# Regrouping a weight conversion beside a pooled attention: four visits per head pair behind the two result bursts, and doubled staging buffers

## The chip, the cores and the metric

One core of a Trainium2 chip runs the kernel. The metric is the device time of one execution in microseconds (us), median of the runs shown. Engines are called PE (TensorE), DVE (VectorE), ACT (ScalarE), POOL (GpSimd) and SP (SyncE, which here only issues DMAs).

## The reference, cut to what matters

```python
B, H, S, D = 8, 8, 1152, 64            # q, k, v: float32
q_pool = q.reshape(B, H, 576, 2, D).mean(axis=3)
scores = q_pool @ k.T / 8              # 576 x 1152 for each head
attn = softmax(scores)                 # stable: the row's maximum is subtracted
x = heads_side_by_side(attn @ v)       # 8 x 576 x 512
theta = x @ w_theta                    # 512 x 512
y = w_tok_r @ (x * cos(theta)) + w_tok_i @ (x * sin(theta))   # 576 x 576 each
u = x + y
out = u + relu(u @ w_ch)               # w_ch 512 x 512
```

The four weights arrive as float64. [...]

## The kernel before, in words

The kernel has two phases. Phase 1 is the attention, 32 pairs of heads (`NPAIR`); phase 2 is the rest, batch by batch. This case is about phase 1.

A pair has 18 positions, two halves `u` of nine `escore` steps. One step is eight short matmuls into a PSUM slot `pe` and an exponential by ACT (`pc`). PSUM has four slots (`bank2`), handed out in an order fixed when the program is written. The matmuls of later pairs are mixed in: `maxpass` (PE writes a slot `pm`, DVE reduces it to row maxima, `mx`), twelve times a pair. POOL adds the exponentials (`ssum`). Twice a pair comes a burst (`AV_AT`): 36 matmuls `pa` that multiply the exponentials with V.

- The burst of u = 0 stands at position 10.35. Ahead of its 36 matmuls PE transposes inputs of pair i+2 (`pt`); ACT makes the high part `hi`, DVE the low part `lo`. Behind them ACT copies the result (`xu`) and PE sums for the norm (`pns`). Call the place behind it A.
- The burst of u = 1 stands at 19.25, that is 1.25 of the next pair. Ahead of its matmuls come transposes for pair i+3 and `max_tail`, whose maxima DVE takes (`px`), then `hi` by ACT and `lo` by DVE. Call the place behind it C.

The row maxima next to C are at positions 2.45, 3.65 and 4.5 of a pair, next to A at 11.1, 12.35 and 13.45. Between burst and maxima stand `norm_out` (DVE, 10.5), `norm_store` (SP, 10.6), `norm_recip` (DVE, 1.5), `norm_save` and `norm_bcast` (SP, 1.6 and 1.7).

All engines run in the order of these positions: every function is put into a list with `at(position, priority, ...)`, the list is sorted, and each engine executes its instructions in just this order.

The weights are 18 blocks of up to 128 rows: four of `w_theta`, four of `w_ch`, five each of `w_tok_r` and `w_tok_i`, in turn. They go through a generator `wgen` that is advanced one step at each position in `W_AT`, nine a pair (20 a pair in the last two, `W_LAST`). A block takes 15 or 16 steps, so 1.7 pairs: fetch by DMA (`raw`), six DVE operations (L545 shift, L548 mask, L550 maximum, L552 shift and mask, L556 merge, L560 mask) with an ACT conversion (L547) behind the first, two POOL operations (L562, L564), nearly each in a step of its own; then the end: for `square` blocks a copy by ACT and a subtraction by POOL, for `token` blocks five PE transposes into a slot `pw`, two ACT copies and two DVE subtractions (L184). The staging tiles `raw`, `ws`, `wf` exist once.

Of the kernel before, what the change touches and what calls it, by code (L numbers as in the profile page):

```python
# [9 lines left out]
F32 = mybir.dt.float32  # L10
F32R = mybir.dt.float32r
# [3 lines left out]
ALU = mybir.AluOpType  # L15
# [5 lines left out]
MAX_AT = (-24.9, -23.65, -22.55, -20.85, -19.55, -18.8, -15.55, -14.35, -13.5, -11.6, -10.2, -9.15)  # L21
SS_LAG = 4.5
AV_AT = (10.35, 19.25)
W_FIRST = (9.45, 9.5, 9.85, 10.5, 12.75, 18.0, 18.6, 19.25, 20.45)
W_AT = (9.45, 9.5, 9.85, 10.5, 12.75, 18.0, 18.6, 19.25, 20.45)
W_LAST = (9.4, 10.2, 11.0, 11.8, 12.6, 13.4, 14.2, 15.0, 15.8, 16.6, 17.4, 18.2, 19.0, 19.8, 20.6, 21.4, 22.2, 23.0, 23.8, 24.6)
W_END = 30
PRO = ((-34.75, -25.8, -18.2), (-6.0, -5.0, 3.15), (3.75,))
MAX_AT0 = (-25.75, -25.25, -24.75, -24.25, -24.15, -23.25, -22.0, -21.95, -21.75, -21.25, -20.75, -20.25)
MAX_AT1 = (-18.1, -16.8, -16.1, -15.35, -14.7, -14.0, -13.3, -12.6, -11.7, -10.3, -9.8, -9.0)  # L30
# [61 lines left out]
TINY = 2.0**-15  # L92
# [9 lines left out]
def pooled_attention_moe_kernel(  # L102
# [24 lines left out]
    ND = DM // P  # L127
# [80 lines left out]
    with ExitStack() as p1:  # L208
# [305 lines left out]
            del state[i]  # L514

        def weights():
            wst = pw.enter_context(tc.tile_pool(name="wst", bufs=1, side="right"))
            wide = w_theta.dtype != F32

            def words(w):  # L520
# [2 lines left out]
                return w.bitcast(U32).rearrange("r (e o) -> r e o", o=2)  # L523

            def fetch(parts, n):
                ws = wst.tile([P, SQ], F32, tag="ws", name="ws")
# [5 lines left out]
                return raw, ws  # L532

            def narrow(raw, ws, R, n, g):
                dst = ws[0:R, 0:n].rearrange("a (t p) -> a p t", t=g)
                if not wide:
                    nc.vector.tensor_copy(
                        dst, raw[0:R, 0:n, 0].rearrange("a (p t) -> a p t", t=g)
                    )
                    return  # L540
                lo, hi = raw[0:R, 0:n, 0], raw[0:R, 0:n, 1]
                f = wst.tile([P, SQ], U32, tag="wf", name="wf")[0:R, 0:n]
                tl = lo.bitcast(F32)
                mk = ws[0:R, 0:n]
                nc.vector.tensor_scalar(lo, lo, 8, None, ALU.logical_shift_right)  # L545
                yield
                nc.scalar.activation(tl, lo, AF.Copy, scale=2.0**-44)  # L547
                nc.vector.tensor_scalar(f, hi, 0x7FFFFFFF, None, ALU.bitwise_and)  # L548
                yield
                nc.vector.tensor_scalar(mk, f.bitcast(F32), TINY, None, ALU.max)  # L550
                yield
                nc.vector.tensor_scalar(  # L552
                    f, mk.bitcast(U32), 3, 0x3FFFFFF8, ALU.logical_shift_left, ALU.bitwise_and
                )
                yield
                nc.vector.scalar_tensor_tensor(  # L556
                    f, hi, 0xC0000000, f, ALU.bitwise_and, ALU.bitwise_or
                )
                yield
                nc.vector.tensor_scalar(hi, f, 0xFF800000, None, ALU.bitwise_and)  # L560
                yield
                nc.gpsimd.tensor_tensor(tl, tl, hi.bitcast(F32), ALU.mult)  # L562
                yield
                nc.gpsimd.tensor_tensor(  # L564
                    dst,
                    f.bitcast(F32).rearrange("a (p t) -> a p t", t=g),
                    tl.rearrange("a (p t) -> a p t", t=g),
                    ALU.add,
                )
                yield  # L570

            def split_slow(hi, lo, src, eng):
                nc.scalar.copy(hi, src)
                yield
                eng.tensor_tensor(lo, src, hi.bitcast(F32), ALU.subtract)
                yield

            def square(wv, c, dst):
                yield
                raw, ws = fetch([(slice(0, P), wv[:, c])], DM)  # L580
                yield
                yield
                yield from narrow(raw, ws, P, DM, 1)
                yield
                if dst is None:
                    hl = [wst.tile([P, DM], F32R, tag=f"hl{n}", name="hl") for n in range(2)]
                    yield from split_slow(hl[0], hl[1], ws[:, 0:DM], nc.gpsimd)
                    yield
                    for n in range(2):
                        nc.sync.dma_start(wcd[n][c], hl[n].bitcast(F32))  # L590
                else:
                    yield from split_slow(dst[0][:, c], dst[1][:, c], ws[:, 0:DM], nc.gpsimd)
                yield

            def token(wv, kb, jt):
                R = P if jt < 4 else HT
                yield
                raw, ws = fetch([(dst, wv[t, ps]) for dst, t, ps in segments(jt)], SQ)
                yield
                yield  # L600
                yield from narrow(raw, ws, R, SQ, QT)
                yield
                yield
                yield
                pw2 = bank2("pw", "pwt")
                pt = pw2[:, 0]
                ra = 0 if kb == 0 else HT
# [14 lines left out]
                for dst, src in (  # L622
                    (
                        [w[:, kb : kb + 4, cs] for w in wtk],
                        pt.rearrange("a (j c) -> a j c", c=P)[:, :, 0:R],
                    ),
                    ([w[ra:rz, 8, cs] for w in wtk], ph[ra:rz, 0:R]),
                ):
                    split(dst[0], dst[1], src, nc.scalar, nc.vector)
                yield  # L630

            jobs = []
            for w, dst in ((w_theta, wth), (w_ch, None)):
                wv = words(w).rearrange("(c p) e o -> p c e o", p=P)
                jobs.append([square(wv, c, dst) for c in range(ND)])
            for w, kb in ((w_tok_r, 0), (w_tok_i, 4)):
                wv = words(w).rearrange("(p t) s o -> t p s o", t=QT)
                jobs.append([token(wv, kb, jt) for jt in range(5)])
            for n in range(5):
                for group in jobs:  # L640
                    if n < len(group):
                        yield from group[n]

        def early():
            run(wgen)
# [61 lines left out]
        pw = ExitStack()  # L707
# [4 lines left out]
            if c < ND - 1:  # L712
                at(XHI0_AT + 0.01 * c, 10, xlo, 0, c)
        for i in range(NPAIR):
            for pos in W_FIRST if i == 0 else W_AT if i < W_END else W_LAST:
                at(NU * i + pos, 10, next, wgen, None)
        for _, _, _, fn, args in sorted(todo, key=lambda e: e[:3]):
            fn(*args)
# [292 lines left out]
```

## Time and profile before

| | us |
|---|---|
| runs | 1395.92, 1396.42, 1396.66 (median 1396.42) |
| the profiled execution | 1395.23 |
| its span, first to last instruction | 1393.2 |
| granted clock over the span | 0.996 |

The profiled execution is longer than its span by 2.0 us, which lie outside the program's instructions. The attention takes the first 890 us or so of the span. Busy shares of the span are PE 96%, DVE 62%, ACT 52%, POOL 66%. "Busy" of an engine says little of a bound when an engine's instructions overlap each other; the waits and the starts of the bursts say more.

### The profile page before, as it was taken

The numbers are of one execution on the slowest core, as the hardware profiler recorded it, in microseconds if no ns is written. First come the engines' busy times: TensorE is split into PE (matmuls) and PEld (weight loads), VectorE is DVE, ScalarE is ACT, GpSimd is POOL, SyncE is SP. The second block draws the span as 40 slices with busy tenths as digits, with TensorE's granted clock in tenths as the row PEclk, the third lists the DMA queues.
The fourth block names the chain that finished last, engine by engine and source line by source line (L and its number), as shares of the span: only waits on it lengthen the run. The fifth ranks groups of instructions, "written<-read, shape, count | busy, mean of one in ns | idle before, by whom it ended". The sixth has DMA issues, their size and how long they took to land.

```text
span 1393.2 us, 29952 instructions
## 1 busy us (share of the span) xinstructions
PE 1342.4 (96%) x12178; PEld 1088.3 (78%) x12178; DVE 864.6 (62%) x1143; ACT 724.0 (52%) x1250; POOL 914.4 (66%) x672
## 2 busy tenths in 40 slices
PE   5999999999999999999999999899999999999998
PEld 3777777776777677777777777698999999999998
DVE  5867776776667776777677765465363453535442
ACT  1556565565556555565555565365454444445341
POOL 1789888989898998889898898742332322233220
PEclk9999999999999999999999999999999999999999
DMA  4334343334433444333443333221111211111111
GB/s 102 101 87 117 89 110 103 110 100 117 110 85 96 114 115 106 93 111 85 128 112 87 82 83 99 74 78 39 35 46 35 62 42 35 39 35 46 27 35 35
DMA packets 130906, 111.66 MB, mean 80 GB/s; under 512 B 95040, under 2 KB 95424, under 8 KB 130768
## 3 DMA queue, kind: packets, MB, share of 16 engines
q1 hardware_dynamic: 130592, 109.28, 28.9%
q8 instruction: 96, 1.57, 0.5%
q0 software_dynamic: 176, 0.46, 0.1%
q14 instruction: 42, 0.34, 0.1%
HBM read 88.29 MB, written 21.27 MB: 79 GB/s over the span
## 4 chain that ended last, share of the span: by engine, by line
PE 72%; DVE 15%; ACT 7%; DMA 3%; issue 2%; POOL 1%; SPq 0%; ACTq 0%; POOLq 0%; DVEq 0%
PE pe L390 18%; PE pa L411 17%; PE py L841 11%; PE pth L763 7%; PE pr L880 6%; DVE mx L332 5%; PE pt L285 4%; PE pm L325 3%; PE pns L427 2%; ACT pc L393 2%; PE pxn L751 1%; DVE r L785 1%; DVE r L786 1%; PE po L903 1%; DVE mx L351 1%
## 5 line engine op out<-in xcount | busy, mean ns | idle before, releaser
L402 POOL TENSOR_TENSOR ss<-ss,pc 128x576 f32<-128x576 f32 x384 | 561.8, 1463 | 68.9 <-ACT pc L393 45.8
L332 DVE TENSOR_REDUCE mx<-pm 128x2 f32<-128x768 f32 x384 | 347.5, 951 | 125.6 <-PE pm L325 124.0
L393 ACT ACTIVATE pc<-pe 128x576 f32<-128x576 f32 x576 | 364.8, 652 | 98.2 <-PE pe L390 85.6
L411 PE MATMUL pa<-pc,vn 128*64 128x288 f32 x2304 | 293.5, 409 | 0.9 <-PE pmt L362 0.8
L814 POOL TENSOR_TENSOR Z<-ab,Z 128x512 fp32r<-128x512 f32 x40 | 51.6, 1291 | 309.4 <-ACT Z L810 274.1
L411 PEld LDWEIGHTS pa<-pc,vn 128*64 128x64 f32 x2304 | 162.2, 137 | 109.4 <-issue 5.4
L841 PE MATMUL py<-wtk,Z 128*128 128x288 f32 x1728 | 242.0, 297 | 0.0
L841 PEld LDWEIGHTS py<-wtk,Z 128*128 128x128 f32 x1728 | 233.2, 189 | 1.5 <-ACT Z L810 0.2
L390 PE MATMUL pe<-hi 64*128 64x288 f32 x1152 | 202.7, 345 | 12.3 <-DVE mx L332 7.3
L390 PEld LDWEIGHTS pe<-hi 64*128 64x128 f32 x1152 | 109.5, 184 | 83.2 <-ACT pc L393 34.0
L390 PE MATMUL pe<-nmr,oner 64*128 64x288 f32 x1152 | 171.9, 291 | 2.2 <-DMA nmr<-mT 2.2
L390 PE MATMUL pe<-lo,hi 64*128 64x288 f32 x1152 | 172.2, 293 | 0.0
L390 PE MATMUL pe<-hi,lo 64*128 64x288 f32 x1152 | 172.0, 292 | 0.0
L325 PE MATMUL pm<-hi 64*128 64x384 f32 x768 | 137.5, 354 | 9.1 <-DVE mx L332 4.7
L390 PEld LDWEIGHTS pe<-nmr,oner 64*128 64x128 f32 x1152 | 110.5, 185 | 2.6 <-DMA nmr<-mT 2.6
L390 PEld LDWEIGHTS pe<-lo,hi 64*128 64x128 f32 x1152 | 111.0, 186 | 0.0
L390 PEld LDWEIGHTS pe<-hi,lo 64*128 64x128 f32 x1152 | 110.4, 185 | 0.0
L312 DVE TENSOR_TENSOR lo<-pt,hi 128x768 fp32r<-128x768 f32 x64 | 67.6, 1056 | 64.5 <-ACT hi L301 64.5
L880 PEld LDWEIGHTS pr<-us,wch 128*128 128x128 f32 x768 | 104.5, 188 | 2.0
L880 PE MATMUL pr<-us,wch 128*128 128x288 f32 x768 | 105.8, 295 | 0.0
L301 ACT CAST hi<-pt 128x768 fp32r<-128x768 f32 x64 | 56.2, 878 | 84.4 <-DVE mx L352 68.1
L402 POOL TENSOR_TENSOR ss<-pc,pc 128x576 f32<-128x576 f32 x64 | 93.8, 1466 | 5.9 <-ACT pc L393 5.9
(105 smaller groups left out, 1657.9 us busy)
## 6 DMA issues: line engine op xcount, KB each, us to landing
qn<-in_q_dram SPq DMA_DIRECT2D x32, 576.0 KB
kn<-in_k_dram SPq DMA_DIRECT2D x64, 288.0 KB
vn<-in_v_dram SPq DMA_DIRECT2D x32, 576.0 KB
dn<-ro SPq DMA_DIRECT2D x64, 144.0 KB
xd<-xu SPq DMA_DIRECT2D x32, 288.0 KB
xT<-xd SPq DMA_DIRECT2D x8, 1152.0 KB
out_dram<-on SPq DMA_DIRECT2D x23, 192.0 KB
out_dram<-on SPq DMA_DIRECT2D x23, 128.0 KB
```

Source lines behind the costliest of these rows:

```text
L285: nc.tensor.transpose(out=pt[:, n, c : c + R], in_=src.rearrange("p h d -> p (h d)"), identity=ident[0:R, 0:R],)
L301: nc.scalar.copy(hi, src)
L312: nc.vector.tensor_tensor(lo, src, hi.bitcast(F32), ALU.subtract)
L325: nc.tensor.matmul(pm[:, h, 0:W], hi[hs, Q0 + j * P : Q0 + (j + 1) * P], hi[hs, K0[3 * g] : K0[3 * g] + W], start=True, stop=True,)
L332: nc.vector.tensor_reduce(mx[:, j : j + 5 : 4, g : g + 1], pm[:, :, 0:W], AX.X, ALU.max)
L390: nc.tensor.matmul(pe[:, h, 0:HALF], w[hs], x[hs], start=(n == 0), stop=(n == 3))
L393: nc.scalar.activation(pcs[u, kt], pe[:, :, 0:HALF], AF.Exp, scale=SC)
L402: nc.gpsimd.tensor_tensor(st["ss", u], first, st["pc"][u, kt], ALU.add)
L411: nc.tensor.matmul(pa[hs, 0, 0:HALF], st["vn"][:, h, kt, :], st["pc"][u, kt][:, h, :], start=(kt == 0), stop=(kt == KT - 1),)
L763: nc.tensor.matmul(th, xs[c][:, j * P : (j + 1) * P], ws[:, c], start=(n == 0), stop=(n == 11))
L841: nc.tensor.matmul(st["py", c, u][:, 0:HALF], Z[zi][:, c * P : (c + 1) * P], wtk[wi][:, kw, u * HALF : (u + 1) * HALF], start=(i == 0 and ...
L880: nc.tensor.matmul(pr[u][:, 0:HALF], wch[wi][:, c, e * P : (e + 1) * P], st["us", ui][:, c, u * HALF : (u + 1) * HALF], start=(n == 0), st ...
```

## The change

- Four visits a pair, at 10.4 and 12.0 (A, and half a position behind one more `escore`) and at 19.3 and 20.9 (C, and the same behind it), take the place of nine, in all pairs alike.
- A block takes six visits (1.5 pairs). Its first: DVE operations shift, mask and maximum together, and the fetch of the next block. Its third: the ACT conversion and the other three DVE operations. Its fifth: both POOL operations. The second, fourth and sixth hold nothing of this.
- The end of a block runs beside the next block's visits: the ACT copy (or the PE transposes and both ACT copies) at that block's first visit, a token's DVE subtractions at its second, a square's POOL subtraction at its third.
- `raw`, `ws` and `wf` are doubled, and a block is fetched one block ahead.

The visits alternate: a block's first, third and fifth visits all fall to A or C. Blocks 0, 2, 4, ... have them at C, A, C; blocks 1, 3, 5, ... at A, C, A.

```diff
-W_FIRST = (9.45, 9.5, 9.85, 10.5, 12.75, 18.0, 18.6, 19.25, 20.45)
-W_AT = (9.45, 9.5, 9.85, 10.5, 12.75, 18.0, 18.6, 19.25, 20.45)
-W_LAST = (9.4, 10.2, 11.0, 11.8, 12.6, 13.4, 14.2, 15.0, 15.8, 16.6, 17.4, 18.2, 19.0, 19.8, 20.6, 21.4, 22.2, 23.0, 23.8, 24.6)
-W_END = 30
+W_AT = (10.4, 12.0, 19.3, 20.9)
...
-            wst = pw.enter_context(tc.tile_pool(name="wst", bufs=1, side="right"))
+            wst = pw.enter_context(tc.tile_pool(name="wst", bufs=2, side="right"))
...
                 nc.vector.tensor_scalar(lo, lo, 8, None, ALU.logical_shift_right)
+                nc.vector.tensor_scalar(f, hi, 0x7FFFFFFF, None, ALU.bitwise_and)
+                nc.vector.tensor_scalar(mk, f.bitcast(F32), TINY, None, ALU.max)
                 yield
                 nc.scalar.activation(tl, lo, AF.Copy, scale=2.0**-44)
-                nc.vector.tensor_scalar(f, hi, 0x7FFFFFFF, None, ALU.bitwise_and)
-                yield
-                nc.vector.tensor_scalar(mk, f.bitcast(F32), TINY, None, ALU.max)
-                yield
                 nc.vector.tensor_scalar(
                     f, mk.bitcast(U32), 3, 0x3FFFFFF8, ALU.logical_shift_left, ALU.bitwise_and
                 )
-                yield
                 nc.vector.scalar_tensor_tensor(
                     f, hi, 0xC0000000, f, ALU.bitwise_and, ALU.bitwise_or
                 )
-                yield
                 nc.vector.tensor_scalar(hi, f, 0xFF800000, None, ALU.bitwise_and)
                 yield
                 nc.gpsimd.tensor_tensor(tl, tl, hi.bitcast(F32), ALU.mult)
-                yield
                 nc.gpsimd.tensor_tensor(
...
+            def square(c, dst, ws):
...
+                nc.scalar.copy(hl[0], src)
                 yield
                 yield
-                yield from narrow(raw, ws, P, DM, 1)
+                nc.gpsimd.tensor_tensor(hl[1], src, hl[0].bitcast(F32), ALU.subtract)
+                yield
                 yield
                 if dst is None:
...
+                for (hi, lo), src in parts:
+                    nc.scalar.copy(hi, src)
                 yield
+                for (hi, lo), src in parts:
+                    nc.vector.tensor_tensor(lo, src, hi.bitcast(F32), ALU.subtract)
...
+            def step(steps):
+                steps[:] = [g for g in steps if next(g, "end") != "end"]
+
+            raws = [fetch(blocks[0][0], blocks[0][2])]
+            yield
+            yield
+            for n, (parts, R, cols, g, end) in enumerate(blocks):
+                step(ends)
+                ws = wst.tile([P, SQ], F32, tag="ws", name="ws")
+                body = narrow(raws[n], ws, R, cols, g)
+                next(body)
+                if n + 1 < len(blocks):
+                    raws.append(fetch(blocks[n + 1][0], blocks[n + 1][2]))
+                yield
+                step(ends)
+                yield
+                for _ in range(2):
+                    step(ends)
+                    next(body, None)
+                    yield
+                    step(ends)
+                    yield
+                ends.append(end(ws))
+            for _ in range(8):
+                step(ends)
+                yield
...
-            for pos in W_FIRST if i == 0 else W_AT if i < W_END else W_LAST:
+            for pos in W_AT:
                 at(NU * i + pos, 10, next, wgen, None)
```

## Rows read from the trace of the kernel before

**Rows 1.** The profile page, part 4: the chain of work that ended last, by engine.

```profile
PE 72%; DVE 15%; ACT 7%; DMA 3%; issue 2%; POOL 1%; SPq 0%; ACTq 0%; POOLq 0%; DVEq 0%
```

**Rows 2.** The same chain in order of time, whole span, pieces of bursts only: start in us, length in us, what. Those at 74.96, 127.45, 396.95, 425.68 and 831.41 are bursts of u = 0 (74.96 that of pair 1, 831.41 that of pair 29), the others of u = 1.

```profile
74.96 4.52 PE pa L411 x36
...
115.12 4.52 PE pa L411 x36
127.45 4.52 PE pa L411 x36
141.20 4.52 PE pa L411 x36
...
167.70 4.52 PE pa L411 x36
181.14 4.59 PE pa L411 x36
...
396.95 4.52 PE pa L411 x36
412.21 4.52 PE pa L411 x36
425.68 4.51 PE pa L411 x36
439.41 4.51 PE pa L411 x36
...
831.41 4.52 PE pa L411 x36
```

**Rows 3.** The timeline of DVE behind the burst at 115.12 (C, no weight operation near): start, length, instruction, and idle time before it with what ended it.

```profile
117.39 0.96 DVE L312 TENSOR_TENSOR lo<-pt,hi 128x768 fp32r<-128x768 f32 x1 [0.86 <-ACT hi L301]
118.26 0.20 DVE L451 RECIPROCAL rc<-rc 128x9 f32<-128x9 f32 x1
120.58 2.69 DVE L332 TENSOR_REDUCE mx<-pm 128x2 f32<-128x768 f32 x3 [2.12 <-PE pm L325]
```

**Rows 4.** The timeline of DVE behind the bursts at 412.21 and at 790.9 (both C), where a weight operation stands between the first row maximum and the second.

```profile
418.54 1.45 DVE L545 TENSOR_SCALAR raw<-raw 128x512 uint32<-128x512 uint32 x1
419.91 1.81 DVE L332 TENSOR_REDUCE mx<-pm 128x2 f32<-128x768 f32 x2
...
799.20 1.81 DVE L332 TENSOR_REDUCE mx<-pm 128x2 f32<-128x768 f32 x2
```

**Rows 5.** The timeline of PE in the same two places: the wait behind the first of them, and the burst before and after the second.

```profile
420.91 0.40 PE L390 MATMUL pe<-hi 64*128 64x288 f32 x2 [1.22 <-DVE mx L332]
...
790.92 0.95 PE L411 MATMUL pa<-pc,vn 128*64 128x288 f32 x6
...
804.90 0.70 PE L411 MATMUL pa<-pc,vn 128*64 128x288 f32 x3
```

**Rows 6.** Groups of instructions by line and shape, whole span: times found | busy us, mean ns of one | idle us before them, and what ended it. Six DVE operations of a block of 576 columns, then the ACT conversion, a token's larger DVE subtraction, `norm_out`, and POOL's sums.

```profile
L545 DVE TENSOR_SCALAR raw<-raw 128x576 uint32<-128x576 uint32 x8 | 6.7, 840 | 7.6 <-DMA raw<-in_moe_w_tok_i_dram 5.4 <-POOL ss L402 2.3
L548 DVE TENSOR_SCALAR wf<-raw 128x576 uint32<-128x576 uint32 x8 | 9.4, 1173 | 0.0
L550 DVE TENSOR_SCALAR ws<-wf 128x576 f32<-128x576 f32 x8 | 10.6, 1330 | 0.1
L552 DVE TENSOR_SCALAR wf<-ws 128x576 uint32<-128x576 uint32 x8 | 9.5, 1184 | 0.1
L556 DVE SCALAR_TENSOR_TENSOR wf<-raw,wf 128x576 uint32<-128x576 uint32 x8 | 11.8, 1480 | 0.1
L560 DVE TENSOR_SCALAR raw<-wf 128x576 uint32<-128x576 uint32 x8 | 5.4, 670 | 0.1
L547 ACT ACTIVATE raw<-raw 128x576 f32<-128x576 uint32 x8 | 5.9, 735 | 2.3 <-DVE raw L545 2.1
L184 DVE TENSOR_TENSOR wtk<-pwt,wtk 128x512 fp32r<-128x512 f32 x8 | 5.5, 691 | 10.8 <-ACT wtk L181 10.8
L473 DVE TENSOR_TENSOR xu<-xu,dn 128x576 f32<-128x576 f32 x32 | 35.8, 1119 | 15.2 <-DMA dn<-ro 15.2
L402 POOL TENSOR_TENSOR ss<-ss,pc 128x576 f32<-128x576 f32 x384 | 561.8, 1463 | 68.9 <-ACT pc L393 45.8
```

**Rows 7.** The timeline of DVE, three weight operations in a row ahead of the burst at 560.2 and one during the burst at 615.1, and that of POOL, the operation that waits for the latter one with its idle time before.

```profile
559.17 1.04 DVE L545 TENSOR_SCALAR raw<-raw 128x576 uint32<-128x576 uint32 x1
560.13 1.67 DVE L548 TENSOR_SCALAR wf<-raw 128x576 uint32<-128x576 uint32 x1
561.84 1.55 DVE L550 TENSOR_SCALAR ws<-wf 128x576 f32<-128x576 f32 x1
...
616.27 0.43 DVE L560 TENSOR_SCALAR raw<-wf 128x512 uint32<-128x512 uint32 x1
...
616.78 1.04 POOL L562 TENSOR_TENSOR raw<-raw 128x512 f32<-128x512 f32 x1 [1.56 <-DVE raw L560]
```

**Rows 8.** Busy time of the engines in six stretches of 4.2 to 4.3 us each that begin 3.2 to 3.3 us (C) or 2.1 us (A) behind the start of a burst, where `lo` ends when no weight operation is ahead of it: the sum and mean over six at C (from 118.35, 253.05, 305.55, 415.45, 632.10 and 686.00), then over six at A (from 129.60, 264.20, 290.70, 427.80, 643.30 and 670.90).

```profile
sum 25.50, PE 25.50 PEld 19.55 DVE 13.80 ACT 14.27 POOL 24.26; mean PE 4.25 PEld 3.26 DVE 2.30 ACT 2.38 POOL 4.04
...
sum 25.20, PE 25.20 PEld 14.01 DVE 13.54 ACT 9.31 POOL 16.06; mean PE 4.20 PEld 2.34 DVE 2.26 ACT 1.55 POOL 2.68
```

**Rows 9.** The timeline of DVE behind the bursts at 396.95 and at 425.68 (both A): `lo` with no weight operation ahead of it, and the third to sixth row maximum behind a weight operation.

```profile
397.88 1.16 DVE L312 TENSOR_TENSOR lo<-pt,hi 128x960 fp32r<-128x960 f32 x1 [1.89 <-ACT hi L301]
...
434.55 3.54 DVE L332 TENSOR_REDUCE mx<-pm 128x2 f32<-128x768 f32 x4
```

More of the change, by code (lines that the diff above doesn't have):

```diff
@@ L525, in fetch @@
             def fetch(parts, n):
-                ws = wst.tile([P, SQ], F32, tag="ws", name="ws")
                 raw = wst.tile(
@@ L531, in fetch @@
                     nc.sync.dma_start(raw[dst, 0:n], src)
-                return raw, ws
+                return raw
             def narrow(raw, ws, R, n, g):
@@ L569, in narrow, with token @@
                 )
[L570 to L580, printed above, removed]
+            def square(c, dst, ws):
+                if dst is None:
+                    hl = [wst.tile([P, DM], F32R, tag=f"hl{n}", name="hl", bufs=1) for n in range(2)]
+                else:
+                    hl = [d[:, c] for d in dst]
+                src = ws[:, 0:DM]
+                nc.scalar.copy(hl[0], src)
                 yield
                 yield
-                yield from narrow(raw, ws, P, DM, 1)
+                nc.gpsimd.tensor_tensor(hl[1], src, hl[0].bitcast(F32), ALU.subtract)
+                yield
                 yield
                 if dst is None:
-                    hl = [wst.tile([P, DM], F32R, tag=f"hl{n}", name="hl") for n in range(2)]
-                    yield from split_slow(hl[0], hl[1], ws[:, 0:DM], nc.gpsimd)
-                    yield
                     for n in range(2):
                         nc.sync.dma_start(wcd[n][c], hl[n].bitcast(F32))
[L591 to L595, printed above, removed]
+            def token(kb, jt, ws):
                 R = P if jt < 4 else HT
[L597 to L604, printed above, removed]
                 pw2 = bank2("pw", "pwt")
@@ L621, in token @@
                 )
-                for dst, src in (
+                parts = (
                     (
@@ L627, in token @@
                     ([w[ra:rz, 8, cs] for w in wtk], ph[ra:rz, 0:R]),
-                ):
-                    split(dst[0], dst[1], src, nc.scalar, nc.vector)
+                )
+                for (hi, lo), src in parts:
+                    nc.scalar.copy(hi, src)
                 yield
+                for (hi, lo), src in parts:
+                    nc.vector.tensor_tensor(lo, src, hi.bitcast(F32), ALU.subtract)
             jobs = []
@@ L634, in weights @@
                 wv = words(w).rearrange("(c p) e o -> p c e o", p=P)
-                jobs.append([square(wv, c, dst) for c in range(ND)])
+                jobs.append(
+                    [
+                        ([(slice(0, P), wv[:, c])], P, DM, 1, lambda ws, c=c, dst=dst: square(c, dst, ws))
+                        for c in range(ND)
+                    ]
+                )
             for w, kb in ((w_tok_r, 0), (w_tok_i, 4)):
                 wv = words(w).rearrange("(p t) s o -> t p s o", t=QT)
[L638 to L642, printed above, removed]
+                jobs.append(
+                    [
+                        (
+                            [(dst, wv[t, ps]) for dst, t, ps in segments(jt)],
+                            P if jt < 4 else HT,
+                            SQ,
+                            QT,
+                            lambda ws, kb=kb, jt=jt: token(kb, jt, ws),
+                        )
+                        for jt in range(5)
+                    ]
+                )
+            blocks = [group[n] for n in range(5) for group in jobs if n < len(group)]
+            ends = []
+            def step(steps):
[18 more added lines that the diff above has]
+                    step(ends)
+                    yield
+                ends.append(end(ws))
+            for _ in range(8):
+                step(ends)
+                yield
         def early():
```

## The prediction, made before the changed kernel ran

> **What bounds the kernel now.** I read the chain of what ended last first. PE holds 72% of it and DVE 15% [rows 1], so the question is where PE waits for DVE. For that the bursts are a ruler: PE cannot start one before all its earlier work is done. Where no weight operation is near, a burst of u = 1 is followed by the next burst after 12.33 us (115.12 to 127.45) and one of u = 0 after 13.75 us (127.45 to 141.20) [rows 2]. A clean pair so takes 26.08 us. From the burst of pair 1 to that of pair 29, 28 pairs, 756.45 us pass [rows 2]; 28 clean pairs would take 730.2. So the weights cost the attention 26.2 us there, and no change of their order can win more than this and what lies outside those pairs.
>
> Part of it is PE's own work. With a token's transposes in it, the stretch from 167.70 to 181.14 took 13.44 us [rows 2], 1.11 more than clean. Nine of the ten tokens lie in these pairs (the tenth in pair 30), about 10 us. The other 16 are waits.
>
> The timelines tell which. Behind a clean burst at C, DVE ends `lo` at 118.35, which is 3.23 us after the burst's start, needs 0.20 for the reciprocal, then idles 2.12 us until PE has the first matmuls for the row maxima ready; the second maximum starts at about 121.5, 6.35 after the burst's start, since three of them take 2.69 [rows 3]. In pair 13 a weight operation of 1.45 us stands between the first and the second: the second starts 7.70 after the burst's start (412.21 to 419.91), 1.35 late [rows 2, 4]. PE then waits 1.22 us, for just that maximum [rows 5], and the next burst comes after 13.47 us instead of 12.33, 1.14 late [rows 2]. In pair 27 the second maximum is 1.86 late (8.28 behind the burst's start in the timeline, which lies 0.07 ahead of the chain's piece), and the next burst comes after 13.98, 1.65 late [rows 4, 5]. Both say the same: at C the second row maximum may be 0.21 us late for nothing, and each us beyond that is a us of the kernel.
>
> **At A there is more room.** In pair 14 the third maximum started 8.87 us behind the burst's start, behind a weight operation [rows 2, 9], and the next burst came after 13.73 us (425.68 to 439.41) [rows 2], no later than clean.
>
> **The change, part by part.** It removes nothing that PE, DVE, ACT or POOL compute. It moves DVE's six operations of a block into two groups of three, each directly behind `lo` at A or C. With six visits a block and four a pair, each block has one of its groups at C and one at A: 18 groups at each place, pairs 0 to 27. It gives up the places ahead of the bursts, where the kernel before did part of this work while PE was not waiting for DVE.
>
> *A group at C.* If a group takes t, the second maximum starts 3.23 + t + 0.20 + 0.90 behind the burst's start, so it is late by t - 2.02, and costs PE t - 2.23. What is t? The three mean durations are 0.84 + 1.17 + 1.33 = 3.34 us, and 1.18 + 1.48 + 0.67 = 3.33 for the other three [rows 6]. But these means include operations that met an idle POOL: one such took 0.43 with POOL idle for 1.56 us up to its end [rows 7]. The nearest row for three in a row beside a busy POOL is the triple at 559.17: 1.04 + 1.67 + 1.55 = 4.26 us [rows 7]. At C POOL is busy 24.26 of 25.50 us in six such stretches [rows 8]. So the bounds are 3 x 0.43 = 1.3 (POOL never in the way) and 4.26; I take 4.0, near the triple, since POOL has short gaps at C too. That is 1.77 us each. One of the 18 lies ahead of pair 1, where both kernels have such a group near C; 17 x 1.77 = 30.1 us.
>
> A rule speaks against this grouping as well. The Trainium skill (SBUF — State Buffer, Who interferes with whom) says that DVE in a two-port mode and GpSimd share a port pair under an exclusive lock, held for a whole instruction, so that the second comer blocks until the first has finished. By this rule every operation of a group waits for a POOL instruction; the durations of 0.43 and 1.67 us for operations of one kind agree with it. By rule in full the sum would be larger; that is the third rival below.
>
> *A group at A.* `lo` ends at 399.04, 2.09 behind the burst's start [rows 2, 9]; then the group, `norm_out` of 1.12 [rows 6], two maxima of 0.90. The third starts at t + 5.01, free up to 8.87, so up to t = 3.86. At A POOL is busy only 16.06 of 25.20 us [rows 8], so t is mostly under that; with 4.26 it costs 0.4. I take 0.1 for each of 18: 1.8 us; bounds 0 and 0.4.
>
> *Tokens.* Five (those of w_tok_r) now stand at A, one (the last) at a C without a group: PE's transposes cost 1.11 each as before, 6.7 us. The four others stand at a C where PE waits for DVE anyway: nothing while the group covers them, 1.11 each without it. But their subtraction stands at position 2.9, between the first and second maximum, and delays the second by 0.69 [rows 6]: 4 x 0.69 = 2.8 us. The second, smaller subtraction may add to that; I leave it to the upper bound.
>
> *ACT.* Its conversion (0.74 [rows 6]) and the copies come behind the result's copy, ahead of the next exponential. At C the wait for DVE hides them. At A the four PSUM slots do, in part; bounds 0 and 0.74 for each of 18; I take 0.1, 2 us.
>
> *POOL, SP and the doubled tiles.* POOL gets the same instructions, two steps later, so it no longer idles for DVE as in the 1.56 us above; it is not the bound, and I take 0. If its two operations in a row held up an exponential, the price would be one POOL sum of 1.46 at most where it happens [rows 6]. On SP the fetch at A stands behind `load_max` and ahead of `norm_store`, and its tile was freed half a pair earlier. `norm_recip` moves behind the group, up to 4.3 us later; on SP `norm_save`, `norm_bcast` and the later load of q wait with it. It has from 118.26 to the `norm_out` behind the next burst at 127.45, over 9 us, so I take 0. `norm_out` moves too, and with it `norm_store`, `load_v`, `norm_spread` and `norm_load`, all needed half a pair later or more.
>
> The Trainium skill (Trainium Kernel Development and Optimization, Best Practices) advises to double-buffer so that DMA and compute overlap. The row shows what there is to win: DVE idled 5.4 us for a token's data in this shape, all in one wait [rows 6]. By the rule the sum would be lower by no more than that; by the row the delay is already among the 16 us of waits that I count as gone.
>
> **The sum.** After: 30.1 + 1.8 + 6.7 + 2.8 + 2 = 43.4 us in place of 26.2, so +17.2. Pair 30 loses its token, -1.1. In all +16.1. The profiled execution took 1395.2, which gives 1411.3; the median of the runs is 1.2 above the profiled one: 1412.5.
>
> **The rivals.**
>
> *The groups at C are short* (faster). If POOL leaves them alone, t = 1.3, under the free 2.23, so C costs nothing; what is left is ten tokens, 11.1, and 2 of ACT: 13.1 instead of 27.3, and 1382. For it: the 0.43 us row. Against it: POOL's 24.26 of 25.50. It decides from t = 3.05 down.
>
> *The mean durations hold.* t = 3.33, 1.10 at each C, 18.7 in place of 30.1: 1401. For it: two of three operations in the other group may find POOL waiting for an exponential, since PE stands. Against: the means come from places with an idle POOL too.
>
> *The lock in full.* Each operation waits for a POOL sum of 1.46, the first for half of one: 0.73 + 2 x 1.46 + 3 x 0.43 = 4.94, so 2.71 at C (+16.0) and 0.4 at A rather than 0.1 (+5.4): 1434. For it: 1.67 and 1.55 for the second and third in the triple. Against: the triple's sum is 4.26. The Trainium skill (SBUF — State Buffer, Who interferes with whom) states such a lock; no row here shows its full price.
>
> *No net change.* t near 3.05, so that C costs 0.82 each, just what the removed waits return: 1394 to 1399.
>
> **How the numbers follow.** Likeliest case (t from 3.6 to 4.4), 1405 to 1424: 0.50, and 1412 is its time. Mean durations, 1399 to 1405: 0.14. Lock in full, above 1424: 0.14. No net change: 0.08. Faster: 0.14. A run of this kernel can tell about 0.2%, 2.8 us. So slower 0.78, same 0.08, faster 0.14. The range 1394 to 1430 leaves out the faster cases and about half of the lock's.
>
> **What the profile of the changed kernel would show.** Right: at C three weight operations behind `lo` with a sum near 4 us, the second maximum 1.5 to 2.2 us late, PE's `pe` waiting for `mx`, the next burst 14 us after such a burst; at A still 13.7 to 14; bursts at C with only the two POOL operations at 12.3. Wrong: groups at C of 3 us or less; or PE waiting at A, for `norm_out` or for an exponential behind ACT's conversion; or POOL's sums so late that exponentials wait.

## The result, and the profile after

The changed kernel takes 1417.15 us (median of four runs, 1415.77 to 1418.25), against 1396.17 us for the kernel before, run beside it. The ratio is 1.015, with a 95% interval from 1.0132 to 1.0167: slower by 21 us. The forecast was 1412, in a range from 1394 to 1430. The profiled execution took 1415.77 us, its span is 1414.0. Ratios below are to the kernel before, run beside each experiment; one run, 1470.92 us at a granted clock of 0.849 in the run of both edits together, was in a slow state and is left out of its median and ratio.

The chain of what ended last, in order of time, places the loss. Its columns are start, length, what; again only pieces of bursts are copied.

```profile
74.74 4.52 PE pa L408 x36
88.64 4.52 PE pa L408 x36
100.97 4.51 PE pa L408 x36
129.25 4.52 PE pa L408 x36
157.66 4.52 PE pa L408 x36
171.62 4.52 PE pa L408 x36
199.90 4.54 PE pa L408 x36
212.57 4.52 PE pa L408 x36
...
852.21 4.52 PE pa L408 x36
```

From the burst of pair 1 (74.74) to that of pair 29 (852.21) 777.47 us pass; it was 756.45 before [rows 2]. That is +21.0. From pair 29's burst to the end of the span it is 561.8 in both kernels, so all of the loss lies in these pairs. Read the pieces like a ruler. A stretch, here and below, goes from the start of one burst to the start of the next. The one without weight operations, 88.64 to 100.97, takes 12.33, as it did before. Pair 3, with a group of three at C (129.25 to 157.66), takes 28.41 in place of 26.08. Pair 4's second burst to pair 5's second burst (171.62 to 199.90) takes 28.28, with a token and a group at A. Behind that, C with a group (199.90 to 212.57) takes only 12.67.

The timeline of DVE shows the group at C behind the burst of u = 1 of pair 3. Columns: start, length, instruction, idle time before it with what ended it.

```profile
146.12 1.39 DVE L543 TENSOR_SCALAR raw<-raw 128x576 uint32<-128x576 uint32 x1
147.43 1.68 DVE L544 TENSOR_SCALAR wf<-raw 128x576 uint32<-128x576 uint32 x1
149.22 1.67 DVE L545 TENSOR_SCALAR ws<-wf 128x576 f32<-128x576 f32 x1
150.81 0.20 DVE L448 RECIPROCAL rc<-rc 128x9 f32<-128x9 f32 x1
150.93 1.76 DVE L329 TENSOR_REDUCE mx<-pm 128x2 f32<-128x768 f32 x2
```

The group, three of the six operations that turn the two 32-bit words of a weight into float32 numbers, holds DVE from 146.12 to 150.81, 4.69 us. It starts right behind `lo`, and the first row maximum only then, at 150.93; a second one follows in the same row. PE's timeline has the price:

```profile
151.88 0.44 PE L322 MATMUL pm<-hi 64*128 64x384 f32 x2 [2.01 <-DVE mx L329]
```

PE waits 2.01 us for that first maximum. POOL's timeline in the same place:

```profile
144.30 2.89 POOL L399 TENSOR_TENSOR ss<-ss,pc 128x576 f32<-128x576 f32 x2
147.15 1.64 POOL L399 TENSOR_TENSOR ss<-pc,pc 128x576 f32<-128x576 f32 x1
149.16 2.98 POOL L399 TENSOR_TENSOR ss<-ss,pc 128x576 f32<-128x576 f32 x2 [0.36 <-ACT pc L390]
```

DVE's operations end at 147.51, 149.11 and 150.89. POOL's sums end at 147.19, 148.79 and, by half of the last row, 150.65: each operation of DVE ends 0.2 to 0.3 us behind a sum. The other kind of group (the last three operations of a block), in pair 5, meets a POOL that idles for most of it. The rows are DVE's, then POOL's.

```profile
203.04 1.47 DVE L548 TENSOR_SCALAR wf<-ws 128x576 uint32<-128x576 uint32 x1
204.54 0.76 DVE L551 SCALAR_TENSOR_TENSOR wf<-raw,wf 128x576 uint32<-128x576 uint32 x1
205.34 0.46 DVE L554 TENSOR_SCALAR raw<-wf 128x576 uint32<-128x576 uint32 x1
```

```profile
206.18 2.92 POOL L399 TENSOR_TENSOR ss<-ss,pc 128x576 f32<-128x576 f32 x2 [1.99 <-ACT pc L390]
```

Here POOL idled 1.99 us for an exponential, and the second and third operation ran in 0.76 and 0.46. The groups by line and shape (times found | busy us, mean ns | idle before) show the mean over the eight larger blocks of 576 columns, at A and C together, where [rows 6] has the kernel before:

```profile
L543 DVE TENSOR_SCALAR raw<-raw 128x576 uint32<-128x576 uint32 x8 | 7.3, 914 | 0.0
L544 DVE TENSOR_SCALAR wf<-raw 128x576 uint32<-128x576 uint32 x8 | 13.4, 1677 | 0.0
L545 DVE TENSOR_SCALAR ws<-wf 128x576 f32<-128x576 f32 x8 | 12.7, 1584 | 0.8
L548 DVE TENSOR_SCALAR wf<-ws 128x576 uint32<-128x576 uint32 x8 | 10.2, 1281 | 0.0
L551 DVE SCALAR_TENSOR_TENSOR wf<-raw,wf 128x576 uint32<-128x576 uint32 x8 | 6.1, 758 | 0.3
L554 DVE TENSOR_SCALAR raw<-wf 128x576 uint32<-128x576 uint32 x8 | 3.7, 463 | 0.3
```

The first three sum to 4.18 us (3.34 before), the other three to 2.50 (3.33 before). For these blocks the grouping made one half dearer and the other cheaper. The idle time for DMA ahead of the first operation, 5.4 us before, is gone. In the kernel before it was one wait, behind the burst of u = 0 of pair 12, and the stretch there took 15.15 us, 1.41 above clean; so no more than about 1.4 us was won by that, and no run shows how much of it.

### The profile page after: what moved, and what is told of

Same layout as the page of the kernel before. It is cut to its first block, busy times and chain, and to the rows that moved or that the text cites. A ratio compares the mean times of both kernels' runs of the same rounds, so it can differ in the third digit from the quotient of the medians.

```text
span 1414.0 us, 29944 instructions
## 1 busy us (share of the span) xinstructions
PE 1346.1 (95%) x12178; PEld 1089.3 (77%) x12178; DVE 871.5 (62%) x1143; ACT 721.6 (51%) x1250; POOL 907.7 (64%) x672
## 4 chain that ended last, share of the span: by engine, by line
PE 69%; DVE 15%; ACT 8%; issue 4%; DMA 2%; POOL 1%; SPq 0%; ACTq 0%; POOLq 0%; DVEq 0%
PE pe L387 19%; PE pa L408 13%; PE py L862 11%; PE pth L784 7%; PE pr L901 5%; PE pt L282 4%; PE pm L322 4%; ACT pc L390 3%; DVE mx L329 2%; PE pns L424 2%; DVE wf L544 1%; DVE mx L348 1%; ACT hi L298 1%; PE px L339 1%; PE pxn L772 1%
## 5 line engine op out<-in xcount | busy, mean ns | idle before, releaser
L399 POOL TENSOR_TENSOR ss<-ss,pc 128x576 f32<-128x576 f32 x384 | 553.3, 1441 | 121.3 <-ACT pc L390 99.2
L322 PE MATMUL pm<-hi 64*128 64x384 f32 x768 | 138.5, 355 | 34.8 <-DVE wtk L610 15.8
L322 PEld LDWEIGHTS pm<-hi 64*128 64x128 f32 x768 | 75.6, 189 | 45.5 <-DVE mx L329 22.4
L399 POOL TENSOR_TENSOR ss<-pc,pc 128x576 f32<-128x576 f32 x64 | 98.7, 1543 | 6.0 <-ACT pc L390 6.0
```

The source lines that it names most:

```text
L322: nc.tensor.matmul(pm[:, h, 0:W], hi[hs, Q0 + j * P : Q0 + (j + 1) * P], hi[hs, K0[3 * g] : K0[3 * g] + W], start=True, stop=True,)
L399: nc.gpsimd.tensor_tensor(st["ss", u], first, st["pc"][u, kt], ALU.add)
```

## The experiments

Two theories stood against each other. Theory: at C the group delays the second row maximum because its operations wait for POOL's sums, so its length is set by POOL. Rival: it is the place or the number of moved operations, or the ends of the blocks (tokens, ACT), with POOL beside the point.

### POOL out of the way, in both kernels

The sums of the four exponentials kt 4 to 7 of u = 1, which POOL makes around C, are left out of the changed kernel, and the same of the kernel before.

```diff
-            if kt == 0 or kt >= TAIL:
+            if kt == 0 or kt >= TAIL or (u == 1 and kt >= 4):
```

> The changed kernel without the sums of the last four exponentials of u = 1 (kt 4 to 7), so the softmax's denominators are not those of the reference; POOL is free of them around C. Theory (a DVE operation of a group takes 0.43 us, and the rest of its 1.4 to 1.7 is waiting for a POOL instruction): groups at C shrink from 3.9 to 4.5 to under 2.5 us, the stretches behind come down to under 12.7 us, and the kernel to 1388 to 1398. Rival (these operations take 1.3 to 1.6 us of DVE's own time): groups and stretches as before, 1413 to 1419.

> The kernel before without the same sums (denominators not those of the reference either): what the omission does by itself. Theory: its waits at C are shorter too, 5 to 12 us less than 1396, so that nearly all of the 21 us between the two kernels is gone when POOL is out of the way. Rival (the difference lies in where the operations stand, whatever POOL does): 1394 to 1397, and the difference between the kernels stays at 21.

Measured: 1388.32 us for the changed kernel without these sums (two runs; 0.9948, 0.9928 to 0.9968), inside the theory's range; 1394.76 for the kernel before without them (0.9989, 0.9978 to 1.0), where the theory (5 to 12 us less) missed. DVE's timeline at C of pair 3 of the changed kernel:

```profile
143.64 0.45 DVE L543 TENSOR_SCALAR raw<-raw 128x576 uint32<-128x576 uint32 x1
...
144.57 0.46 DVE L545 TENSOR_SCALAR ws<-wf 128x576 f32<-128x576 f32 x1
144.94 0.21 DVE L448 RECIPROCAL rc<-rc 128x9 f32<-128x9 f32 x1
145.96 2.69 DVE L329 TENSOR_REDUCE mx<-pm 128x2 f32<-128x768 f32 x3 [0.81 <-PE pm L322]
```

The group takes 1.30 us (143.64 to 144.94) and DVE again waits for PE; the stretch comes down from 14.68 to 12.40 us. The same edit that takes 28.8 us off the changed kernel takes 1.6 off the kernel before. In the profiled executions of the changed kernel 23.0 us of this lie between the bursts of pairs 1 and 29. Another 4.4 lie behind them, where PE no longer waits 4.28 us for POOL's last sums at the end of the attention, and these have nothing to do with the groups; in the kernel before that end gets 3.5 us shorter as well. So the 21 us are not the price of the places by themselves: with POOL out of the way, groups without a token cost 0.1 to 0.2 us each in the same places, and the difference between the kernels doesn't stay at 21, which the rival asked for. For the groups the rival that leaves POOL out falls. For the tokens it holds: the stretches with one behind a burst are still 1.4 to 2.3 us above clean. That the changed kernel is now 6.4 us ahead says less: beside the old places POOL still has other sums to make (at C of pair 3 of the kernel before, two weight operations still take 1.48 and 1.32 us). The experiment does not yet say what DVE and POOL contend for, since leaving sums out also takes work away.

### All of POOL's work, another layout

Here nothing is left out. The scratch tiles of the conversion are laid out as 3 x 192 words with a pitch of 200, while the DMA tile stays one row of 576. A block of 512 columns is filled up to 576 by a small DMA, so DVE works on more columns than before, not fewer. The shift goes to a tile of its own, which ACT's conversion reads, and POOL's last operation goes by the same three pieces; this part of the edit isn't printed.

```diff
-                f = wst.tile([P, SQ], U32, tag="wf", name="wf")[0:R, 0:n]
+                f = wst.tile([P, 3, 200], U32, tag="wf", name="wf")[0:R, :, 0:192]
+                sh = wst.tile([P, 3, 200], U32, tag="wsh", name="wsh")[0:R, :, 0:192]
...
-                nc.vector.tensor_scalar(lo, lo, 8, None, ALU.logical_shift_right)
+                nc.vector.tensor_scalar(sh, lo, 8, None, ALU.logical_shift_right)
...
+                    if n < SQ:
+                        nc.sync.dma_start(raw[dst, n:SQ], src[:, 0 : SQ - n])
```

> The changed kernel with the scratch of a block's conversion laid out as 3 rows of 192 in a pitch of 200, so that input and output of each of its tensor_scalar operations differ in their outermost dimension (3 against 576). The Trainium skill (VectorE: DVE Perf Modes, Mode 2x_2P) grants the two-port mode only where these are both even or equal, so the operations should run at half rate and ask for no port that POOL holds. (Blocks of 512 columns are filled to 576 with 64 of their own.) Theory (the excess at C is waiting for POOL's instruction): the five operations take about 0.7 us each whatever POOL does, a group at C 2.2 to 3.3 us instead of 3.9 to 4.5, the first groups cost nothing there, and the kernel falls by 15 to 25 us to 1392 to 1402. Rival (DVE is slowed by POOL in any mode, or the layout makes them slower): no gain or a loss, 1415 or more, since each operation has twice the work.

Measured: 1393.36 us (0.9981, 0.9972 to 0.9991), 23.8 less than the changed kernel and inside the theory's range. DVE's timeline at C of pair 3:

```profile
144.06 0.74 DVE L548 TENSOR_SCALAR wsh<-raw 128x576 uint32<-128x576 uint32 x1
...
145.57 0.75 DVE L550 TENSOR_SCALAR ws<-wf 128x576 f32<-128x576 f32 x1
146.24 0.20 DVE L448 RECIPROCAL rc<-rc 128x9 f32<-128x9 f32 x1
```

and POOL's beside it, two sums without a gap over the whole of the group:

```profile
143.35 2.95 POOL L399 TENSOR_TENSOR ss<-ss,pc 128x576 f32<-128x576 f32 x2
```

An operation in this layout takes 0.74 us where the same one alone took 0.45 and beside POOL 1.39 to 1.68. It is slower by itself, and the group is 2.18 us long instead of 4.69, just under the 2.23 that the prediction found free. So what is contended for hangs on the layout of an operation's tiles, and not only on POOL's being busy. The Trainium skill (VectorE: DVE Perf Modes, Mode 2×_2P) says that an operation with one source uses both of DVE's read ports and both of its write ports for it when the outermost dimensions of source and destination are both even or equal; here they are 3 and 576. The trace agrees: the duration no longer depends on POOL, all 90 such operations of the run took 0.73 to 0.76 us. That it is a port which DVE and POOL share is the skill's reading; a trace shows only the durations. One operation stays exposed. In the groups by shape the merge, which reads two tiles, has a mean above its neighbour:

```profile
L556 DVE SCALAR_TENSOR_TENSOR wf<-raw,wf 128x576 uint32<-128x576 uint32 x16 | 14.3, 893 | 0.5
L559 DVE TENSOR_SCALAR raw<-wf 128x576 uint32<-128x576 uint32 x16 | 12.1, 754 | 0.6
```

Its single durations go from 0.75 to 1.88 us. The Trainium skill (SBUF — State Buffer, Who interferes with whom) has DVE operations with two SBUF inputs contend with POOL instructions that read SBUF; 893 against 754 ns agrees with it but does not prove it.

The same layout in the kernel before, with its own places:

> The kernel before with the same layout of the scratch as the one-port kernel, its visits as they were. Theory: its nine visits are mostly where PE doesn't wait, and of its 16 us of waits (some 11 at a weight operation of 1.0 to 1.5 us between the first and second row maximum) half an us each is saved: 3 to 8 us less, 1388 to 1393. Rival: 1396 or more.

Measured: 1392.82 (0.9977, 0.9968 to 0.9987), 3.0 less than the kernel before. In the old places the layout wins 3 us, in the new ones 23.8. With it the two orders are within 0.6 us of each other, 1392.82 and 1393.36, so the loss of the change is the price of POOL beside the new places, and the new order, with its tokens where they are, wins nothing.

### The groups ahead of the burst at C

The two visits at C are moved to positions ahead of the burst.

```diff
-W_AT = (10.4, 12.0, 19.3, 20.9)
+W_AT = (10.4, 12.0, 17.25, 18.5)
```

> The changed kernel with its two visits at C (19.3 and 20.9) moved ahead of the burst of u = 1, to 17.25 and 18.5; A stays. Theory (at C a group of three DVE operations keeps the second row maximum waiting, and PE with it): in the changed kernel the 17 stretches behind a burst of u = 1 that hold a group cost about 28 us over clean. Ahead of the burst DVE has some 1.4 us free, so a group of 4.0 to 4.5 us still makes lo some 2.5 us late, and the second maximum 0.3 to 1 us later than is free: 5 to 15 us remain. 1417 falls to 1394 to 1404. Rival (what costs is the grouping itself, wherever it stands: the same DVE time, the same meetings with POOL): within 4 us of the changed kernel, 1413 to 1421.

Measured: 1438.41 (1.0307, 1.029 to 1.0324), a miss of both. The chain's bursts of pair 6, which has a group and a token:

```profile
216.06 4.52 PE pa L408 x36
235.13 5.98 PE pa L408 x36
```

Pair 3, with a group and no token, takes 27.81 (130.22 to 158.03 on the chain) in place of 28.41: only 0.6 won, because `px`'s maxima, `hi` and `lo` now stand behind the group, and the row maxima behind them. What costs is the token of pair 6. From its first burst to its second it is 19.07 us, where the changed kernel needed 14.04. PE's timeline says why:

```profile
234.21 0.82 PE L339 MATMUL px<-hi,tail 128*128 128x512 f32 x3 [4.19 <-DVE wtk L610]
```

`px` needs the PSUM slot of the token's transposes, which DVE's subtraction frees, and that stands behind the weight group on DVE (4.87 us here). Behind this stand of PE the burst itself takes 5.98 instead of 4.52. In the table of windows (busy us of PE, PEld, DVE, ACT and POOL with counts, then PE's granted clock, DMA share, GB/s) its first part ran at a granted clock of 0.50, that is 1.2 GHz:

```profile
235.00:238.00 3.00, 3.00 (x15) 1.48 (x15) 2.07 (x3) 0.80 (x1) 0.77 (x1) 0.50 0.02 5
```

What follows: a group can be moved out of one wait into the next only with all that queues behind it on DVE, and a token's subtraction holds one of four PSUM slots.

### Tokens later, away from the group at A

The ends of the `w_tok_r` blocks are held back by four visits, so that they no longer meet the group at A.

```diff
             def token(kb, jt, ws):
+                for _ in range(4 if kb == 0 else 0):
+                    yield
```

> The changed kernel with the end of the w_tok_r blocks (PE transposes, ACT copies, DVE subtractions) four visits later, so that it meets the visits with only POOL operations and no DVE group. Theory (a token's PSUM slot stays taken until DVE has done the group, norm_out, a row maximum and then the subtraction, and PE's next pm waits for it): the five stretches at A with a token, 11.8 us in the changed kernel where clean ones take 9.55, split into 9.6 to 10.0 with a group alone and 10.6 with the transposes alone; in sum 5 x 0.7 to 1.2 = 3.5 to 6 us less, 1411 to 1414. Rival (the 2.2 us are PE's own transposes and the group's lateness added up, with no slot in it): the same sum in two places, 1416 to 1418.

Measured: 1417.35 (1.0154, 1.0138 to 1.0169): nothing won, as the rival has it in its time, but not for its reason. The timeline of DVE at A of pair 6, where such a token now stands without a group, and PE's row in the same place:

```profile
219.23 0.96 DVE L329 TENSOR_REDUCE mx<-pm 128x2 f32<-128x768 f32 x1 [3.53 <-PE pm L322]
220.10 0.87 DVE L612 TENSOR_TENSOR wtk<-pwt,wtk 128x512 fp32r<-128x512 f32 x2
```

```profile
221.12 0.44 PE L322 MATMUL pm<-hi 64*128 64x384 f32 x2 [1.40 <-DVE wtk L612]
```

DVE was idle for 3.53 us and yet PE waits 1.40 us: the subtraction stands behind the row maximum in DVE's order. From 211.95 to 227.78 on the chain this stretch takes 15.83, 2.08 more than clean, though there is no group in it; with token and group together it was 15.95. So a token behind a burst costs some 2.1 by itself, nearly twice its 1.11 of PE's own work, and the group is not the reason. The group left alone, at A of pair 5, costs 0.75: apart the two cost 2.8 us, together 2.2.

### Tokens at places of their own

The tokens' ends leave the visits: transposes and copies at position 9.2 of a pair, subtractions at 9.3, both ahead of the burst of u = 0. First in the changed kernel alone.

```diff
+T_AT = (9.2, 9.3)
...
-                ends.append(end(ws))
+                (ends if g == 1 else tends).append(end(ws))
...
+            for pos in T_AT:
+                at(NU * i + pos, 10, step, tends)
```

> The changed kernel with the tokens' ends at 9.2 and 9.3 alone, its conversion as it was. Theory: the five tokens at A, 2.2 us each there, cost 1.1; the four at C lay under a group's wait and now cost 1.1 each of their own; the lone one at C 1.1 instead of 1.6. In sum 0 to 6 us less, 1411 to 1417. Rival (the tokens are what makes a group at C long): the C stretches with tokens fall to under 9 us, and the kernel under 1405.

Measured: 1418.24 (1.0159, 1.0144 to 1.0174), above the ranges of both. From the burst of u = 0 of pair 18 to that of pair 19 (548.52 to 577.95 on the chain) it is 29.43 us, where the changed kernel took 28.73 (546.64 to 575.37). The A with a group fell as expected, from 11.8 to 10.3 us between the start of a burst's last matmul and the next burst; but behind C the token's transposes now lie on PE's own path and are paid there in full on top of the group, since the wait for the group comes before them. The cost was moved, not removed.

Then both edits together, the layout and the tokens:

> The same, and the tokens' ends (PE transposes, ACT copies, DVE subtractions) taken out of the visits to places of their own at 9.2 and 9.3, ahead of the burst of u = 0, where DVE has no row maximum to take. Theory (a token behind a burst costs PE 2.1 us at A and 2.3 at C because its PSUM slot waits for a subtraction behind a row maximum; elsewhere 1.1): another 8 to 12 us less than the one-port kernel alone, 1381 to 1393, below the kernel before. Rival (the slot is taken while the burst's own slots are needed, so the cost moves): within 4 us of the one-port kernel alone.

> The one-port kernel with the tokens' ends at 9.2 and 9.3 once more, for an undisturbed trace. Theory: bursts of u = 1 with a group are followed by the next after 12.3 to 13.5 us, those of u = 0 after 13.7 to 14.0, the stretches with a token after 1.0 to 1.2 more; 1381 to 1385.

Measured: 1381.72 (three runs; 0.9903, 0.9886 to 0.9919), and repeated 1382.61 (0.9902, 0.9886 to 0.9919), both inside the theories' ranges. It beats the kernel before by 1%, and the changed kernel by 35 us. The chain of the second run, pair 5 with the first burst of pair 6:

```profile
179.36 4.51 PE pa L409 x36
193.11 4.54 PE pa L409 x36
206.51 4.56 PE pa L409 x36
```

A with a group (179.36 to 193.11) takes 13.75, which is the clean stretch of [rows 2]. C with a group and a token (193.11 to 206.51) takes 13.40, 1.07 more than clean: about PE's transposes (1.11). With short groups and the tokens elsewhere the order of the change beats the kernel before. Whether the old order, given the layout and the tokens' new places, would do as well was not run.

### Doubled staging tiles alone

```diff
-            wst = pw.enter_context(tc.tile_pool(name="wst", bufs=1, side="right"))
+            wst = pw.enter_context(tc.tile_pool(name="wst", bufs=2, side="right"))
```

> The kernel before with its staging tiles doubled and nothing else. Theory (the doubling has no part in the loss; its fetch still comes two steps ahead of its use): within 2 us of 1396. Rival (doubled tiles cost or win something, as the advice to double-buffer has it: up to the 5.4 us in which DVE waited for one token's data): 1391 to 1393, or over 1399.

Measured, in the kernel before: 1395.88 against 1397.25 (0.9991, 0.9982 to 1.0001), no effect that can be told. The doubling is not the cause of the loss, and by itself no gain. DVE's wait for a token's data stays in this run (5.3 us), since the fetch comes no earlier; so it doesn't say what ending that wait is worth.

## Why the prediction was right, and where its sum was off

**The ruler and the mechanism.** The formula "a group of length t at C costs t - 2.23" held. For pair 3 t is 4.69, which gives 2.46; the stretch is 2.37 longer than clean. So it is in all eleven groups at C that stand without a token and at full clock: t goes from 2.58 to 4.69, and each stretch lies 0.09 to 0.10 us under the formula. With the layout t is 2.18 in pair 3, which gives nothing; the thirteen stretches like it have t from 2.18 to 2.61 and are 0.1 to 0.3 us above clean. PE waits for a row maximum, as was said, but not in the place that was said: the prediction had `pe` wait for the second maximum, and in the trace `pm` waits for the first one. The waits list has it, and no wait of 0.3 us or more of `pe` for `mx` is left in these pairs (engine, line, what it waited for: us in total, times, longest):

```profile
POOL ss L399 <- ACT pc L390: 105.3, 60, 6.0
PE pm L322 <- DVE wtk L610: 15.8, 10, 2.0
PE pm L322 <- DVE mx L329: 15.6, 16, 2.0
```

**The sum, term by term.** I worked out the time from the start of a burst's last matmul to the next burst, less the clean one (8.13 at C, 9.55 at A), from the timeline, over the same 28 pairs:

| term | predicted | measured |
|---|---|---|
| 17 groups at C, with four tokens' subtractions | 30.1 + 2.8 | 32.1 |
| 5 tokens at A, with the groups beside them | 5.6 + 0.5 | 10.4 |
| other groups at A, and ACT | 1.3 + 2.0 | 4.1 |
| the lone token at C | 1.1 | 1.6 |
| sum | 43.4 | 48.3 |

The prediction's clean pair was 26.08 from the chain; the stretches here make it 26.04, which is 1.1 us over 28 pairs. By the prediction's ruler the measured sum is 777.47 - 730.24 = 47.2, against 43.4. The difference of 3.8 is that of the forecast's +17.2 to the +21.0 in these pairs.

**Groups at C: near the right total, from unequal parts.** Thirteen of the 17 groups stand without a token. The prediction gave them 13 x 1.77 = 23.0; they cost 20.7, and 18.5 without the clock told of below. Their excess is 2.4 (the first three operations, pairs 3, 9, 15, 21), 1.8 (the other three, pairs 2, 8, 14, 20) and 0.3 to 0.5 (the other three in pairs 5, 11, 17, 23, 26). In the last, the stretch at A ahead of them had run late, exponentials came late, and POOL idled, as at 206.18; POOL's waits for exponentials doubled, from 51.7 us before to 105.3. The token at A is only a part of that: in the run with later tokens, where it is away, the same groups cost 0.73 to 0.75 (1.52 in pair 26), still not the 1.8 of the others. The mean t of the thirteen is 3.74, against the 4.0 taken; the triple of [rows 7], 4.26 us, lay above nine of them. The rival of the lock in full, t = 4.94, was almost met by the 4.69 of the first three, but only there; its 0.4 at A came for the first three alone.

**Taken for the group: tokens at C.** The other four groups (pairs 6, 12, 18, 24) have a token beside them. The prediction gave these stretches 1.77 for the group and 0.69 for the subtraction, 9.9 us in all; they cost 11.4, again 1.1 of it the clock, but not for the group. PE waits there for the token's subtraction, in the changed kernel (first row, pair 6) and in the one without POOL's sums (second row, the same place), where the group takes only 1.13 us:

```profile
234.82 0.44 PE L322 MATMUL pm<-hi 64*128 64x384 f32 x2 [1.58 <-DVE wtk L610]
```

```profile
229.66 0.44 PE L322 MATMUL pm<-hi 64*128 64x384 f32 x2 [1.53 <-DVE wtk L610]
```

The stretch takes 14.69 us in the one and 14.65 in the other, and without POOL's sums the four still cost 9.2 us. So the token, which costs 2.2 to 2.3 us at C, was charged with 0.69, and the group beside it, which was charged with 1.77, added at most 0.4. The two errors nearly cancel.

**Mis-sized: tokens at A.** The prediction charged PE's transposes, 1.11, and took the subtraction at A as free. Measured, each of four such stretches is 2.2 to 2.3 longer (the fifth, in pair 26, 1.45). Alone the group makes 0.75 and the token 2.1, as the runs above show. The term left out is the PSUM slot: the waits list has 15.8 us of `pm` for the token's subtraction, ten waits, five at A and five at C. The row shows it at A of pair 5:

```profile
193.26 0.44 PE L322 MATMUL pm<-hi 64*128 64x384 f32 x2 [1.56 <-DVE wtk L610]
```

The prediction had looked only at how late the subtraction makes the row maxima, not at how late the row maximum makes the subtraction, and whose slot that holds.

**Groups at A** were near the forecast: 0.43 to 0.49 for the first three (0.4 was the upper bound), and 0.17 to 0.24 for the other three, where ACT's conversion stands. But the room at A, t up to 3.86, did not hold everywhere: at A of pair 5 in the run with later tokens a group of 3.6 us costs 0.75, and `norm_out` behind it, taken at its mean of 1.12, takes 1.98.

**Not foreseen: the clock.** Three stretches at C (pairs 15, 20 and 24) are about 1.1 us longer than their like. The windows show one beside pair 3, which had the same wait:

```profile
152.00:156.00 4.00, 4.00 (x50) 3.44 (x52) 3.80 (x5) 2.61 (x4) 3.82 (x4) 1.00 0.23 77
485.30:488.70 3.40, 3.40 (x32) 3.40 (x30) 2.23 (x3) 1.43 (x3) 2.93 (x3) 0.50 0.48 97
```

That makes some 3.3 of the 32.1 at C. In the run with later tokens the stretch of pair 9 fell and that of pair 15 did not, behind the same wait of 2.01 us. Without the clock all groups at C would have come out 4 us under the forecast. So that the whole came within 4 us is partly luck: the groups without a token were forecast 4.5 us too dear, the nine tokens with the groups beside them were forecast at 16.0 us and cost 20.7 at full clock, and the fall of the clock was not in the sum.

**Pair 30.** Its token moved out of it, and 1.1 was taken off for that. From its first burst to its second it did get shorter, 10.60 us against 11.40. But at the end of the attention PE waits for POOL's last sums, and that wait grew from 3.63 us (at 895.48 before) to 4.28 (at 916.12), so that the stretch from pair 29's burst to the end is 561.8 in both. POOL was taken at nothing, and this end is where it isn't. SP, `norm_recip` and the doubled tiles were taken at nothing, and no wait of PE for them shows up.

## What to carry to other kernels

Before grouping an engine's operations, look at what the other engines do in that very place: the price of a group beside a busy POOL was set by POOL's sums (4.69 us), not by the operations (1.30 us alone), and a layout in which each is slower alone (0.74 instead of 0.45) won 23.8 us. When a step is moved, ask not only whom it delays, but what stands ahead of it in its new queue and which slot it holds until it runs: a token behind a burst cost PE 2.1 to 2.3 us, twice what its transposes take. Where two delays lie in one stretch, look which ends last before adding them up. And a mean duration over a whole run belongs to the old places; after a move the mean itself moves, here from 3.34 to 4.18 and from 3.33 to 2.50.

## What the runs showed of the hardware that was not expected

One and the same DVE operation on 128 x 576 words took 0.45 us with POOL idle, 1.4 to 1.7 beside POOL's sums of 1.44 (pair 3 of the changed kernel), and 0.74 in a layout with unequal outermost dimensions, whatever POOL did.

PE's granted clock fell to 0.50 (1.2 GHz) for 3.4 us in the middle of the attention, behind a wait of PE of 2.01 us at pair 15, while the same wait at pair 3 was followed by 1.00 (2.4 GHz). What decides between the two stayed open. The mean clock of the changed kernel, 0.984 against 0.996, misleads: most of the difference lies in the first 40 us (0.50 from 20 to 30), where pair 1's burst still starts no later (74.74 against 74.96).
